# Attention and a mixture of experts on one core: one transpose block is moved to the head of its stage and to another bank, weight staging to POOL's queue, the query scale to ScalarE

## The chip, the core and the metric

The kernel runs on one core of a Trainium2 chip. The core has a matrix engine (TensorE, "PE" in the profile; its weight loads are listed apart as "PEld"), a vector engine (VectorE, "DVE"), an activation engine (ScalarE, "ACT"), a general engine (GpSimd, "POOL") and a sync engine (SyncE, "SP") that issues transfers; POOL issues transfers too. Engines run their own instructions in order and wait for each other through semaphores. PE writes its results into banks of an accumulator memory (PSUM), which VectorE and ScalarE read. The metric is the time of one execution in microseconds (us), as the device counts it.

## The reference

Causal attention by blocks of 64 over 8 batches of 8 heads, 576 positions, 64 values a head; its output rows, 512 wide, go through a layer of 8 experts with one expert to a row.

```python
scores = scale * np.matmul(q, k.transpose(0, 1, 3, 2))        # scale = 1/8
scores = np.where(block_i >= block_j, scores, -1e9)           # blocks of 64
attn = np.exp(scores - max); attn /= sum + 1e-9
attn_out = np.matmul(attn, v)                                 # x: rows of 8 heads, 4608 x 512
logits = x @ w_gate + modality_bias[modality_id]
e_idx = argmax(logits); gate_w = softmax(logits)[e_idx]
out[e_idx == e] = gate_w * (relu(x @ w1[e]) @ w2[e])
```

## The kernel before

**Attention** works on 32 pairs of heads, four pairs to a batch ("group" below). The program is written in 33 slots; slot s runs the steps of `ORDER` by hand, each engine taking its own steps in that order. A step's second number says how many pairs back it works: `("S0", 0)` is of pair s, `("Va", 1)` of pair s - 1, `("L", -2)` loads pair s + 2.

- `S0` to `S3`: scores (PE, line 197), 64x64 weights, into banks 0 to 5 by `PIECES`; `M0` to `M4`: row maxima (VectorE, 205 and 207); `E0` to `E4`: exponentials into `pm` (ScalarE, 213). `E4` reads banks 4 and 5 and is the last of the slot.
- `G`, `g`: the gate's products with v, and their copy; `L`: the load of a pair's queries and keys into `raw` (SP, 170). `Va`, `Vb` (PE, 247): the transposed weights of the pair before times v; `Za`, `Zb` (VectorE, 259 to 262): division and rows out; after every fourth pair two stores to `xrows` (SP, 265).
- `T0` to `T6` (PE, 223): transposes of `pm` in seven groups, the banks by `GBANK`; `T6` is the single block of the first 64 rows. `C0` to `C6` (228): copies out of the banks into `pt`, groups 1, 3 and 5 on VectorE, the others on ScalarE.
- `q...`: places where one step of a group's routing is run, of a list of 20 (logits, one-hot, counts, positions in the experts' row lists); `qp` takes steps that are small matmuls, `qv` those of VectorE that read them. Behind the routing of group 4 stand 22 further VectorE steps (`choose`, kind "c"), which pick the experts and the first rows.

`scale` multiplies a pair's queries by 1/8 into `q` (line 179): on POOL, at the start of the slot before the one that needs them. A slot's start also issues the loads of v (`load_v`, SP) and up to two scatters of list positions to `idlist` (POOL, 365), if any wait in `placing`.

**Early steps** of the experts lie in attention's last slots (`EARLY_STEPS`). `stage` loads a chunk of weights (128x1024; w1 in two halves) into one of two `staging` tiles; `prep` casts the oldest staged chunk on POOL (553), subtracts the cast from it for the low part (`lower`, 614) and stages the next. `ids` reads row numbers from `idlist` (SP, 626) after the scatters before it; `fetch` gathers rows of `xrows` (POOL, 634); `flush` issues all waiting scatters. Slot 32 (`LAST`) mixes the end of attention with the first expert products.

**Experts** (`run_all`): segments of 256 rows, each with transposes, w1 products (665), relu, w2 products (711) and scatters of the result (714, POOL), while further weight chunks are staged and converted (`convert`).

Of the kernel before, what the change touches and what calls it, by code (L numbers as in the profile page):

```python
# [16 lines left out]
ALU = mybir.AluOpType  # L17
# [5 lines left out]
B, H, S, D = 8, 8, 576, 64  # L23
# [31 lines left out]
    ((3, 0), (3, 1), (2, 0), (1, 0)), ((6, 3), (4, 2), (2, 1), (8, 4)), ((0, 0),),  # L55
)
HALF = 5
GBANK = (0, 1, 2, 3, 4, 5, 0)
POS = {x: 512 * g + 128 * i for g, group in enumerate(GROUPS) for i, x in enumerate(group)}
ON_DVE = (1, 3, 5)  # L60
PARTS = (("idf", (128,)), ("ii", (128,)), ("iom8", (NE,)), ("iom40", (5, NE)), ("iov40", (5, NE)), ("inv5", (5,)), ("first5", (NE, 5)), ("base8", (NE,)), ("edges", (N // SLOT,)))

ORDER = (
# [3 lines left out]
)  # L67

EARLY_STEPS = {
    (25, "S0"): ("ids", "stage", "stage"),  # L70
    (26, "S0"): ("prep",), (26, "T0"): ("prep",),
    (27, "S0"): ("prep",), (27, "T0"): ("prep",),
    (28, "S0"): ("prep",), (28, "T0"): ("prep",),
    (29, "S0"): ("prep",), (29, "T0"): ("prep",),
    (30, "S0"): ("fetch",),
    (31, "S0"): ("fetch",),
# [27 lines left out]
def attention_moe(ctx, tc, qk, vr, vt, gmw, mid, mb, w1, w2, cf, ci, ld, out):  # L104
# [71 lines left out]

    def scale(p):
        d = pairs[p]
        (pool if p else dve).tensor_scalar(d.q, d.raw[:, 0:S], SCALE, None, ALU.mult)  # L179

    def place(s, a, b):
        i, o = COL[s] if a == 0 else (COL[s][0] + 1, -CUT)
# [47 lines left out]
    def gates(p):  # L230
        d = pairs[p]
        for j in range(5):
            for i in range(2 if j < 4 else 1):
                k = 128 * j + 64 * i
                pe.matmul(b0[64 * i : 64 * i + 64, GATE + 2 * NE * j : GATE + 2 * NE * j + 2 * NE], d.vt[:, k : k + 64], gm[:, p % PPB, :], start=True, stop=True)
# [179 lines left out]

    def emit(name, p):
        one = {
            "L": lambda: load(p), "G": lambda: gates(p), "g": lambda: keep_gates(p), "Va": lambda: values(p, 0, SEVEN), "Vb": lambda: values(p, SEVEN, NSUB),
            "Za": lambda: rows(p, o0, 0, SEVEN), "Zb": lambda: rows(p, b0, SEVEN, NSUB),
        }  # L420
        if name in one:
            one[name]()
        else:
            dict(S=scores, M=maxima, E=exps, T=transposes, C=copies)[name[0]](p, int(name[1:]))
# [36 lines left out]
    def run_slot(slot):  # L461
        nonlocal steps, ex
        if slot < NPAIR - 1:
            load_v(slot + 1)
            scale(slot + 1)
        if placing and slot < NPAIR:
            for _ in range(2):
                if placing:
                    g, c = placing.pop(0)
                    g(c)  # L470
        for name, stage in LAST if slot == NPAIR else ORDER:
            p = slot - stage
            for what in EARLY_STEPS.get((slot, name), ()):
                if ex is None:
                    ex = Experts(ctx, tc, cst, scratch, btmp, con["edges"], xrows, idlist, idf, w1, w2, out, sel, run, base8, pick, dot, banks, (o0, banks[5]), placing, staging, extra, xrb)
                ex.early(what)
            if name[0:6] == "+steps":
                for f in steps[0 : int(name[6:])]:
                    f()
                steps = steps[int(name[6:]) :]  # L480
                continue
            if name[0] == "+":
                ex.early(name[1:])
                continue
            if name[0] == "q":
                kind = "" if name[1].isdigit() else name
                if slot > 1 and steps and getattr(steps[0], "kind", "") in ((kind, "c") if not kind else (kind,)):
                    steps.pop(0)()
                    if not kind and steps and getattr(steps[0], "kind", "") == "c":
                        steps.pop(0)()  # L490
                continue
            if not 0 <= p < NPAIR:
                continue
            emit(name, p)
            if name == "Zb" and p % PPB == PPB - 1:
                for f in steps:
                    f()
                steps = routing(p // PPB)
                if p // PPB == EARLY - 1:
                    choose(Later(dve, steps))  # L500
# [18 lines left out]
class Experts:  # L519
# [77 lines left out]
    def stage(self):  # L597
        if not self.todo:
            return
        k, name, c = self.todo.pop(0)  # L600
        st = self.staging[self.sturn % 2]
        self.sturn += 1
        if k == 0:
            for i in range(2):
                self.nc.sync.dma_start(st[64 * i : 64 * i + 64], self.source(k, name, c, i))
        else:
            st = st.rearrange("p (a f) -> p a f", a=2)
            self.nc.sync.dma_start(st, self.source(k, name, c))
        self.staged.append((st, k, name, c))

    def lower(self, on_pool=False):
# [254 lines left out]
```

## Time and profile before

| | us |
|---|---|
| median of 3 runs | 787.83 |
| lowest and highest of them | 787.63, 788.76 |
| the profiled execution | 790.35 |
| its span, first to last instruction | 788.7 |
| mean granted clock of TensorE | 0.988 |

Rows and timelines below are of the profiled execution, in us from the start of its span. A matmul's duration contains its way through the array, so matmuls that follow each other overlap; weight loads run beside matmuls. "issue" as the cause of an idle time means that the profile shows nothing that was waited for. A releaser is inferred, and of several it is the last one by the profile.

### The profile page before, as it was taken

The numbers are of one execution on the slowest core, as the hardware profiler recorded it, in microseconds if no ns is written. First come the engines' busy times: TensorE is split into PE (matmuls) and PEld (weight loads), VectorE is DVE, ScalarE is ACT, GpSimd is POOL, SyncE is SP. The second block draws the span as 40 slices with busy tenths as digits, with TensorE's granted clock in tenths as the row PEclk, the third lists the DMA queues.
The fourth block names the chain that finished last, engine by engine and source line by source line (L and its number), as shares of the span: only waits on it lengthen the run. The fifth ranks groups of instructions, "written<-read, shape, count | busy, mean of one in ns | idle before, by whom it ended". The sixth has DMA issues, their size and how long they took to land. (4 is left out here: it accounts for less than half of the span.)

```text
span 788.7 us, 20741 instructions
## 1 busy us (share of the span) xinstructions
PE 752.3 (95%) x8696; PEld 670.4 (85%) x8696; DVE 369.3 (47%) x1059; ACT 306.5 (39%) x654; POOL 216.5 (27%) x177
## 2 busy tenths in 40 slices
PE   8999999999989888799999999999999999999995
PEld 5888888888878876598999999999998889998894
DVE  6888888888879867654122111122212222212120
ACT  5666666666656654432222221222212222222221
POOL 2111323232323267621732322322222102112100
PEclk9999999999999999899999999999999999999998
DMA  8487565656554667623232112222122122121000
GB/s 236 120 224 218 142 166 144 168 148 165 148 161 126 179 176 225 159 67 85 48 92 81 63 46 81 68 81 68 54 81 81 54 68 68 54 68 45 27 14 19
DMA packets 82625, 85.11 MB, mean 108 GB/s; under 512 B 53003, under 2 KB 64971, under 8 KB 82529
## 3 DMA queue, kind: packets, MB, share of 16 engines
q1 hardware_dynamic: 75040, 64.24, 29.7%
q0 software_dynamic: 7488, 19.52, 7.8%
q8 instruction: 69, 1.13, 0.6%
q14 instruction: 28, 0.22, 0.1%
HBM read 62.09 MB, written 22.25 MB: 107 GB/s over the span
## 5 line engine op out<-in xcount | busy, mean ns | idle before, releaser
L672 DVE SCALAR_TENSOR_TENSOR extra<-bank,extra 128x512 fp32r<-128x512 f32 x72 | 49.8, 692 | 309.0 <-ACT extra L671 308.9
L213 ACT ACTIVATE pm<-bank,nm 128x320 f32<-128x320 f32 (+3 forms) x320 | 138.1, 507 | 89.7 <-DVE nm L205 88.2
L205 DVE TENSOR_REDUCE nm<-bank 128x1 f32<-128x256 f32 (+7 forms) x288 | 111.2, 446 | 39.4 <-PE bank L197 39.2
L665 PE MATMUL bank<-extra 128*128 128x256 f32 x960 | 117.7, 283 | 0.6 <-DVE extra L651 0.3
L665 PEld LDWEIGHTS bank<-extra 128*128 128x128 f32 x960 | 116.6, 192 | 1.7 <-DVE extra L651 0.5
L197 PE MATMUL bank<-raw,q 64*64 64x256 f32 (+7 forms) x1280 | 91.5, 426 | 19.9 <-POOL q L179 10.9
L179 POOL TENSOR_SCALAR q<-raw 128x576 f32<-128x576 f32 x31 | 51.2, 1650 | 212.7 <-DMA raw<-qk 124.5
L671 ACT ACTIVATE extra<-bank 128x512 fp32r<-128x512 f32 x72 | 43.1, 598 | 158.1 <-PE bank L665 158.1
L197 PEld LDWEIGHTS bank<-raw,q 64*64 64x64 f32 x1280 | 61.3, 138 | 49.0 <-issue 31.5
L223 PE MATMUL bank<-cf,pm 128*128 128x128 f32 (+1 forms) x800 | 94.8, 275 | 0.4 <-ACT pm L213 0.4
L665 PE MATMUL bank<-extra,w0hb 128*128 128x256 f32 x512 | 91.2, 281 | 0.0
L223 PEld LDWEIGHTS bank<-cf,pm 128*128 128x128 f32 (+1 forms) x800 | 85.8, 135 | 3.3 <-ACT pm L213 0.8
L228 ACT COPY pt<-bank 128x512 f32<-128x512 f32 (+1 forms) x128 | 62.7, 505 | 46.1 <-PE bank L223 46.1
L665 PEld LDWEIGHTS bank<-extra,w0hb 128*128 128x128 f32 x512 | 79.1, 188 | 0.7
L247 PE MATMUL o<-v,pt 128*64 128x73 f32 x2048 | 75.3, 228 | 1.6 <-issue 1.6
L247 PEld LDWEIGHTS o<-v,pt 128*64 128x64 f32 x2048 | 70.4, 136 | 1.8 <-issue 1.7
L665 PE MATMUL bank<-extra,w0lb 128*128 128x256 f32 x256 | 71.9, 281 | 0.0
L228 DVE COPY pt<-bank 128x512 f32<-128x512 f32 (+1 forms) x96 | 64.9, 684 | 9.5 <-PE bank L223 8.5
L714 POOL DMA_INDIRECT out<-scratch,ids_b x17 | 16.9, 994 | 162.2 <-ACT scratch L713 162.2
L711 PE MATMUL o<-extra 128*128 128x512 f32 x240 | 57.2, 394 | 0.0
L711 PE MATMUL bank<-extra 128*128 128x512 f32 x240 | 56.0, 389 | 0.0
L711 PEld LDWEIGHTS bank<-extra 128*128 128x128 f32 x240 | 45.1, 188 | 9.3
(144 smaller groups left out, 865.7 us busy)
## 6 DMA issues: line engine op xcount, KB each, us to landing
raw<-qk SPq DMA_DIRECT2D x31, 576.0 KB, 4.6
v<-vr SPq DMA_DIRECT2D x32, 320.0 KB, 5.4
vt<-vt SPq DMA_DIRECT2D x32, 288.0 KB, 5.3
xrows<-xr SPq DMA_DIRECT2D x16, 576.0 KB, 6.9
staging<-w SPq DMA_DIRECT2D x24, 256.0 KB, 3.9
staging<-w SPq DMA_DIRECT2D x12, 512.0 KB, 3.8
idlist<-btmp SPq DMA_DIRECT2D x8, 304.0 KB, 5.6
idlist<-idt,pi POOLq DMA_INDIRECT x40, 2.2
```

Of the source, the lines that this page charges most:

```text
L179: (pool if p else dve).tensor_scalar(d.q, d.raw[:, 0:S], SCALE, None, ALU.mult)
L197: pe.matmul(place(s, a, b)[64 * t : 64 * t + 64], d.q[hs, D * s : D * s + D], d.k[hs, a:b], start=True, stop=True)
L205: dve.tensor_reduce(low, place(s, a, b), AX.X, ALU.max, negate=True)
L213: act.activation(d.pm[:, OFF[s] + a : OFF[s] + b], place(s, a, b), AF.Exp, bias=d.nm[:, s : s + 1], scale=1.0)
L223: pe.transpose(banks[GBANK[g]][0:m, 128 * i : 128 * i + 128], d.pm[:, o : o + m], idf)
L228: dve.tensor_copy(dst, src) if g in ON_DVE else act.copy(dst, src)
L247: pe.matmul(o[64 * h : 64 * h + 64], d.pt[:, a : a + 64], d.v[:, 5 * h + j, :], start=j == 0, stop=j == s // 2)
L665: nc.tensor.matmul(hp[:, a, :], w[:, kc, ms], x[:, kc, :], start=i == 0, stop=i == len(mm) - 1)
L671: self.nc.scalar.activation(hh, hp, AF.Relu)
L672: self.nc.vector.scalar_tensor_tensor(hl, hp, 0.0, hh, ALU.max, ALU.subtract)
L711: nc.tensor.matmul(y, s.hs[m][x][:, ts], self.part(w, 1, m // 2)[:, m % 2, :], start=n == 0, stop=n == len(mm) - 1)
L714: nc.gpsimd.indirect_dma_start(self.out, bass.IndirectOffsetOnAxis(ap=s.ids[:, s.t + i : s.t + i + 1], axis=0), yo, None, bounds_check=N - ...
```

## The change

Four edits.

1. `T6` stands first among the transposes and writes bank 5 (`GBANK`); `C6` follows it.
2. `scale` of pairs 1 to 31 runs on ScalarE, as step `("Q", -1)` behind `E4`, that is, for the next pair; POOL no longer scales.
3. `stage` issues its loads from POOL's queue. `ids` moves from slot 25 to slot 28, behind a `flush`.
4. A `q` place takes one step; in the slots of group 5 (20 to 23, `EARLY`) it takes two.

```diff
-GBANK = (0, 1, 2, 3, 4, 5, 0)
+GBANK = (0, 1, 2, 3, 4, 5, 5)
...
-    ("G", 0), ("L", -2), ("q1", 1), ("Va", 1), ("g", 0), ("E4", 0), ("q2", 1), ("q3", 1), ("Vb", 1), ("Za", 1), ("q4", 1), ("Zb", 1),
...
+    ("G", 0), ("L", -2), ("q1", 1), ("Va", 1), ("g", 0), ("E4", 0), ("Q", -1), ("q2", 1), ("q3", 1), ("Vb", 1), ("Za", 1), ("q4", 1), ("Zb", 1),
+    ("T6", 0), ("C6", 0), ("T0", 0), ("C0", 0), ("T1", 0), ("C1", 0), ("T2", 0), ("C2", 0), ("q5", 1), ("T3", 0), ("C3", 0), ("T4", 0), ("C4", 0), ("T5", 0), ("C5", 0), ("qp", 1), ("q6", 1),
...
-    (25, "S0"): ("ids", "stage", "stage"),
+    (25, "S0"): ("stage", "stage"),
...
-    (28, "S0"): ("prep",), (28, "T0"): ("prep",),
+    (28, "S0"): ("flush", "ids", "prep"), (28, "T0"): ("prep",),
...
     def scale(p):
         d = pairs[p]
-        (pool if p else dve).tensor_scalar(d.q, d.raw[:, 0:S], SCALE, None, ALU.mult)
+        if p == 0:
+            dve.tensor_scalar(d.q, d.raw[:, 0:S], SCALE, None, ALU.mult)
+        else:
+            act.mul(d.q, d.raw[:, 0:S], SCALE)
...
             load_v(slot + 1)
-            scale(slot + 1)
...
-                if slot > 1 and steps and getattr(steps[0], "kind", "") in ((kind, "c") if not kind else (kind,)):
-                    steps.pop(0)()
-                    if not kind and steps and getattr(steps[0], "kind", "") == "c":
+                kinds = (kind,) if kind else ("", "c")
+                for _ in range(1 if kind or slot // PPB != EARLY else 2):
+                    if slot > 1 and steps and getattr(steps[0], "kind", "") in kinds:
                         steps.pop(0)()
...
-                self.nc.sync.dma_start(st[64 * i : 64 * i + 64], self.source(k, name, c, i))
+                self.nc.gpsimd.dma_start(st[64 * i : 64 * i + 64], self.source(k, name, c, i))
...
-            self.nc.sync.dma_start(st, self.source(k, name, c))
+            self.nc.gpsimd.dma_start(st, self.source(k, name, c))
```

In what follows a row of the program's order is a line, an operation, output<-input and the output's size; the changed file has its lines 2 or 3 lower. First PE, from the transposes of slot 1 to the scores of slot 2 (`bank_90` to `bank_95` are banks 0 to 5). Before:

```order
L223 MATMUL bank_90<-cf,pm_108 128x128 x4
L223 MATMUL bank_91<-cf,pm_108 128x128 x4
L223 MATMUL bank_92<-cf,pm_108 128x128 x4
L223 MATMUL bank_93<-cf,pm_108 128x128 x4
L223 MATMUL bank_94<-cf,pm_108 128x128 x4
L223 MATMUL bank_95<-cf,pm_108 64x128 x4
L223 MATMUL bank_90<-cf,pm_108 64x128
L197 MATMUL bank_90<-raw_98,q_100 64x512 x2
```

With the change:

```order
L226 MATMUL bank_95<-cf,pm_108 64x128
L226 MATMUL bank_90<-cf,pm_108 128x128 x4
L226 MATMUL bank_91<-cf,pm_108 128x128 x4
L226 MATMUL bank_92<-cf,pm_108 128x128 x4
L226 MATMUL bank_93<-cf,pm_108 128x128 x4
L226 MATMUL bank_94<-cf,pm_108 128x128 x4
L226 MATMUL bank_95<-cf,pm_108 64x128 x4
L200 MATMUL bank_90<-raw_98,q_100 64x512 x2
```

The single block has gone from the last to the first place and from bank 0 to bank 5, so that twenty transposes now lie between the last write to bank 0 and the next scores, which write it first.

Second ScalarE in slot 1, from its last four exponentials to the first of slot 2. Before:

```order
L213 ACTIVATE pm_108<-bank_94,nm 128x256 x2
L213 ACTIVATE pm_108<-bank_95,nm 128x320
L213 ACTIVATE pm_108<-bank_95,nm 128x128
L228 COPY pt_110<-bank_90 128x512
L228 COPY pt_110<-bank_92 128x512
L228 COPY pt_110<-bank_94 128x512
L228 COPY pt_110<-bank_90 64x128
L213 ACTIVATE pm_107<-bank_90,nm 128x512
```

With the change:

```order
L216 ACTIVATE pm_108<-bank_94,nm 128x256 x2
L216 ACTIVATE pm_108<-bank_95,nm 128x320
L216 ACTIVATE pm_108<-bank_95,nm 128x128
L182 ACTIVATE q_100<-raw_98 128x576
L231 COPY pt_110<-bank_95 64x128
L231 COPY pt_110<-bank_90 128x512
L231 COPY pt_110<-bank_92 128x512
L231 COPY pt_110<-bank_94 128x512
L216 ACTIVATE pm_107<-bank_90,nm 128x512
```

Between the last exponential and the copies stands now the scale of the next pair, and the 64x128 copy has gone from the last to the first of the copies.

Third SP's queue from slot 25's raw load on (`raw` loads pairs 27, 28; an ISA row sets an address). Before:

```order
L170 DMA raw_99<-qk 128x1152
L174 DMA vt_103<-vt 128x576
L175 DMA v_104<-vr 128x10x64
L605 ISA
L605 DMA staging_77<-w 64x1024
L605 ISA
L605 DMA staging_77<-w 64x1024
L170 DMA raw_98<-qk 128x1152
L605 ISA
L605 DMA staging_78<-w 64x1024
L605 ISA
L605 DMA staging_78<-w 64x1024
```

With the change, from slot 27's raw load (pair 29) to slot 28's (pair 30) and the stores that follow:

```order
L170 DMA raw_99<-qk 128x1152
L174 DMA vt_103<-vt 128x576
L175 DMA v_106<-vr 128x10x64
L627 TENSOR_LOAD di_a
L628 ISA
L628 DMA ids_lead<-idlist 128x6x1
L170 DMA raw_98<-qk 128x1152
L268 DMA xrows<-xr_79 64x9x256 x2
```

The stagings are gone from between the loads; the row ids of slot 28 now stand ahead of its raw load. The stagings stand on POOL. POOL before, from the scale of pair 29 to the preps of slot 29:

```order
L179 TENSOR_SCALAR q_101<-raw_99 128x576
L365 DMA idlist<-idt,pi 38912x16 x2
L553 CAST extra<-staging_77 128x1024
L614 TENSOR_TENSOR extra<-staging_77,extra 128x1024
L553 CAST extra<-staging_78 128x1024
L614 TENSOR_TENSOR extra<-staging_78,extra 128x1024
L179 TENSOR_SCALAR q_100<-raw_98 128x576
L365 DMA idlist<-idt,pi 38912x16 x2
```

With the change, from the preps of slot 27 to the first of slot 28:

```order
L555 CAST extra<-staging_77 128x1024
L616 TENSOR_TENSOR extra<-staging_77,extra 128x1024
L610 ISA
L610 DMA staging_77<-w 128x2x512
L555 CAST extra<-staging_78 128x1024
L616 TENSOR_TENSOR extra<-staging_78,extra 128x1024
L610 ISA
L610 DMA staging_78<-w 128x2x512
L368 DMA idlist<-idt,pi 38912x16 x5
L555 CAST extra<-staging_77 128x1024
L616 TENSOR_TENSOR extra<-staging_77,extra 128x1024
L610 ISA
```

Each lowering is followed by the transfer of the chunk after next, no scale is left, and the five scatters of slot 28's flush stand between the preps.

## Rows read from the trace of the kernel before

**Rows 1.** One line of the page: busy time of each engine, its share of the span, and its instructions.

```profile
PE 752.3 (95%) x8696; PEld 670.4 (85%) x8696; DVE 369.3 (47%) x1059; ACT 306.5 (39%) x654; POOL 216.5 (27%) x177
```

**Rows 2.** Busy time by stage. Columns: the stretch, its length, then for each engine busy time and (instructions), the granted share of TensorE's clock, the DMA engines' mean busy share, GB/s.

```profile
60.00:200.00 140.00, 135.22 (x2590) 120.28 (x2587) 118.60 (x383) 88.73 (x216) 38.64 (x30) 1.00 0.61 165
200.00:260.00 60.00, 56.10 (x1067) 49.24 (x1066) 51.31 (x178) 36.37 (x88) 18.47 (x15) 1.00 0.55 146
260.00:345.00 85.00, 70.47 (x1190) 60.06 (x1189) 61.17 (x183) 42.50 (x102) 49.47 (x35) 0.92 0.64 171
345.00:740.00 395.00, 395.00 (x2654) 360.58 (x2654) 86.00 (x170) 94.61 (x151) 94.79 (x83) 1.00 0.21 65
```

**Rows 3.** The timeline of slot 3 and of the start of slot 4. Columns: start, duration, engine, line, operation, output<-input, how many in a row, and in brackets the engine's idle time before and what ended it.

```profile
33.62 2.70 PE L197 MATMUL bank<-raw,q 64*64 64x512 f32 x40 [0.39 <-POOL q L179]
...
36.24 0.60 PEld L235 LDWEIGHTS b<-gm,vt 128*64 128x64 f32 x17 [0.17 <-issue]
...
36.38 0.33 SPq L170 DMA_DIRECT2D raw<-qk  x1
...
38.28 1.59 ACT L213 ACTIVATE pm<-bank,nm 128x256 f32<-128x256 f32 x4
...
40.17 2.68 PEld L223 LDWEIGHTS bank<-cf,pm 128*128 128x128 f32 x25
40.17 2.95 PE L223 MATMUL bank<-cf,pm 128*128 128x128 f32 x25
...
42.61 0.81 ACT L228 COPY pt<-bank 128x512 f32<-128x512 f32 x2 [0.23 <-PE bank L223]
43.12 0.68 DVE L228 COPY pt<-bank 64x512 f32<-64x512 f32 x1 [0.25 <-PE bank L223]
43.48 0.24 PEld L197 LDWEIGHTS bank<-raw,q 64*64 64x64 f32 x8 [0.63 <-issue]
43.52 2.70 PE L197 MATMUL bank<-raw,q 64*64 64x512 f32 x40 [0.40 <-issue]
...
44.70 1.82 DVE L205 TENSOR_REDUCE nm<-bank 128x1 f32<-128x512 f32 x4 [0.90 <-PE bank L197]
```

**Rows 4.** The costliest groups of the page, one row: the score matmuls; behind the bar, PE's idle time before them and what ended it.

```profile
L197 PE MATMUL bank<-raw,q 64*64 64x256 f32 (+7 forms) x1280 | 91.5, 426 | 19.9 <-POOL q L179 10.9
```

**Rows 5.** The timeline of PE alone from 250 to 345 us: the routing's small matmul at the end of slot 24, a stall within slot 26, the first scores of slots 27, 28, 30 and 31, and the first transposes of the expert stage.

```profile
254.07 0.44 PE L288 MATMUL b<-l,cf 128*128 128x72 f32 x2 [0.85 <-DVE l L285]
...
271.46 0.28 PE L247 MATMUL o<-v,pt 128*64 128x73 f32 x2 [1.57 <-issue]
...
276.23 2.70 PE L197 MATMUL bank<-raw,q 64*64 64x512 f32 x40 [0.34 <-issue]
...
288.05 4.38 PE L197 MATMUL bank<-raw,q 64*64 64x512 f32 x40 [2.33 <-POOL q L179]
...
312.23 4.39 PE L197 MATMUL bank<-raw,q 64*64 64x512 f32 x40 [2.95 <-POOL q L179]
...
329.43 4.41 PE L197 MATMUL bank<-raw,q 64*64 64x512 f32 x40 [5.24 <-POOL q L179]
...
340.99 1.09 PE L647 MATMUL bank<-cf,xr 128*128 128x128 f32 x8 [0.35 <-ACT pt L228]
```

**Rows 6.** The timeline of all engines in slot 30 and at the start of slot 31: staging and raw load on SP's queue (SPq), the scale on POOL, the scores on PE.

```profile
318.22 1.28 SPq L605 DMA_DIRECT2D staging<-w  x2
...
319.60 0.52 SPq L170 DMA_DIRECT2D raw<-qk  x1
...
327.72 1.65 POOL L179 TENSOR_SCALAR q<-raw 128x576 f32<-128x576 f32 x1 [6.11 <-DMA raw<-qk]
...
329.43 1.12 PE L197 MATMUL bank<-raw,q 64*64 64x512 f32 x4 [5.24 <-POOL q L179]
```

**Rows 7.** Busy time behind the wait of slot 28, columns as in rows 2.

```profile
288.60:291.90 3.30, 3.30 (x34) 2.13 (x30) 1.82 (x4) 1.44 (x4) 3.21 (x3) 0.50 0.02 5
```

**Rows 8.** The timeline of slot 5 (its scores start at 53.41): the last four exponentials, a step of the routing on VectorE, the transposes.

```profile
58.59 1.59 ACT L213 ACTIVATE pm<-bank,nm 128x256 f32<-128x256 f32 x4
...
59.05 0.19 DVE L298 TENSOR_REDUCE mx<-lg 128x5 f32<-128x40 f32 x1
...
60.09 2.95 PE L223 MATMUL bank<-cf,pm 128*128 128x128 f32 x25
```

**Rows 9.** The timeline of slot 0: its first 12 transposes, the last four exponentials, the transposes that waited for one of them.

```profile
9.63 1.53 PE L223 MATMUL bank<-cf,pm 128*128 128x128 f32 x12
...
10.58 1.56 ACT L213 ACTIVATE pm<-bank,nm 128x256 f32<-128x256 f32 x4
...
11.52 1.84 PE L223 MATMUL bank<-cf,pm 128*128 128x128 f32 x13 [0.36 <-ACT pm L213]
```

**Rows 10.** Groups of instructions, by shape: total busy time and mean ns behind the bar. ScalarE's cast of a weight chunk, and POOL's lowering and cast of one.

```profile
L614 POOL TENSOR_TENSOR extra<-staging,extra 128x1024 fp32r<-128x1024 f32 x8 | 18.9, 2362 | 0.7
...
L619 ACT CAST extra<-staging 128x1024 fp32r<-128x1024 f32 x8 | 8.5, 1063 | 0.0
L553 POOL CAST extra<-staging 128x1024 fp32r<-128x1024 f32 x8 | 8.4, 1049 | 0.0
```

**Rows 11.** The list-position scatters on POOL, of the tile pi: shortest, median and longest in ns, and first and last start.

```profile
L365 POOL DMA_INDIRECT idlist<-idt,pi x40: 967/988/1095, 81.8 to 381.5; - x40
```

**Rows 12.** The raw loads that SP issued from 250 to 345 us: time from issue to landing.

```profile
DMA to landing us min/median/max: 4.5/5.7/8.7
```

More of the change, by code (lines that the diff above doesn't have):

```diff
@@ L417, in emit @@
         one = {
-            "L": lambda: load(p), "G": lambda: gates(p), "g": lambda: keep_gates(p), "Va": lambda: values(p, 0, SEVEN), "Vb": lambda: values(p, SEVEN, NSUB),
+            "L": lambda: load(p), "Q": lambda: scale(p), "G": lambda: gates(p), "g": lambda: keep_gates(p), "Va": lambda: values(p, 0, SEVEN), "Vb": lambda: values(p, SEVEN, NSUB),
             "Za": lambda: rows(p, o0, 0, SEVEN), "Zb": lambda: rows(p, b0, SEVEN, NSUB),
```

1 row of the table ORDER is left out of this document.

## The prediction

> **What bounds the kernel now.** I read the page first, then the busy time by stage, then the timeline of one ordinary slot, then the odd slots. TensorE (PE) is busy for 752.3 of 788.7 us [rows 1], and the stages say where the rest is: from 345 to 740 us, the expert stage, it is busy 395.00 of 395 us, so no edit can gain there unless it removes matmuls, and this one removes none. In attention it is busy 135.2 of 140 us, then 56.1 of 60, then, from 260 to 345 us, only 70.5 of 85 with the mean granted clock at 0.92 [rows 2]. So I look for two things: a small wait in every slot, and large ones in the last slots.
>
> The ordinary slot shows the first. It begins with the scores at 33.62 us; the 25 transposes start at 40.17 (6.55 us into the slot), their weight loads end at 42.85 and the matmuls at 43.12; then PE waits 0.40 us (its weight loads 0.63) and the next slot's scores start at 43.52. Of ScalarE's two last copies (0.81 us from 42.61) the second ends at 43.42, just before [rows 3]. In the code that second copy is C6, which frees bank 0, and S0 writes bank 0. So each slot is 9.90 us, and its tail waits for a copy. Summed over slots the first matmul of the scores waited 19.9 us, 10.9 of them for POOL's scaled queries [rows 4].
>
> The second is those queries. In the late slots PE stood 2.33, 2.95 and 5.24 us before the scores of slots 28, 30 and 31, and each time the 40 score matmuls then took 4.38 to 4.41 us, where 2.70 is usual [rows 5]. The reason is SP's queue: weight staging stands in it ahead of the raw load, the staging waits for POOL's lowering of the previous chunk, so the load of slot 31's queries and keys left only at 319.60 us, in slot 30 itself, POOL scaled at 327.72 and PE started at 329.43 [rows 6]. After such a wait the granted clock is 0.50, the 1.2 GHz level [rows 7]; from 60 to 260 us it is 1.00 [rows 2].
>
> **The change, part by part.**
>
> *T6 first, into bank 5.* S0 now waits for C0, done long before, instead of C6. The gap before S0 is 0.40 us by matmuls and 0.63 by weight loads [rows 3]; both are bounds of what a boundary gives. I take 0.55: where nothing holds PE, the gates' weight loads come 0.17 us after those of the scores [rows 3], which leaves 0.46, and the scores may follow closer. 31 boundaries lie before slots 1 to 31; three of them are the query waits, counted below. 28 x 0.55 = 15.4 us. In 13 of these the routing's one or two small matmuls (kind "qp") stood inside the gap at no cost; at about 0.2 us a boundary (two matmuls, issued 0.11 apart as the 25 in 2.95 are) they now cost 2.6. **12.8 us.** The end of the last slot has the same wait, 0.35 us [rows 5]: **0.35**.
>
> What it costs: T6 writes bank 5, so it needs the slot's last exponential (E4), while the first transposes needed only earlier ones. In the ordinary slot E4 ends at 38.28 + 1.59 = 39.87, 0.30 us before the transposes start [rows 3]: covered, as everything else in the slot shifts with the scores. Where "qv" puts three small VectorE operations between the maxima (slots 5, 9, ... 29), E4 ends at 60.18 and the transposes start at 60.09 [rows 8]: with the 0.06 us that lie between the copy's end at 43.42 and the weight load at 43.48, 0.15 x 7 = 1.0 us lost. In slot 0 there is no cover (no values of an earlier pair): transposes began at 9.63, E4 ends at 10.58 + 1.56 = 12.14 [rows 9]. They will start near 12.2 and end 2.95 later at 15.15 instead of 13.36: 1.8 us lost. This opens a gap of 2.57 us; the gaps of 2.33 and more were followed by half clock, the one of 1.57 was not [rows 5], so it may cost another 0 to 1.7 us (the 4.38 less 2.70); I take 0.9. **Together 3.7 us given back.**
>
> *The scale on ScalarE.* POOL took 1.65 us; ScalarE's cast of 128x1024 between SBUF tiles takes 1.06 [rows 10], so 128x576 costs about 0.6. It stands between E4 and C6. ScalarE is busy 88.7 of 140 us [rows 2]; from E4's end (slot time 6.25) the scale ends at 6.9, the transposes' first bank is full at about 7.3, so C0 is not late. Cover: that wait for PE. Without it 0.6 us a slot, 19 us. What is queued behind it, if the raw load is late: all four copies, thus PE. In ordinary slots the load leaves SP at 36.38, 2.8 us into the slot [rows 3], and lands some 6 us later; ScalarE wants it at 9.35 + 6.25 = 15.6, 7 us after that.
>
> *Staging on POOL's queue.* SP then holds only loads of pairs, the xrows stores and the row ids. The raw loads leave in their slot, and the waits of 2.33 + 2.95 + 5.24 = **10.5 us** go, with the slow clock behind them, 1.68 + 1.69 + 1.71 = **5.1 us**. A stall of 1.57 us at 271.46 with no cause in the profile stands just behind the first burst of staging [rows 5]; it may go or stay: **0.8 of it**.
>
> POOL pays: 16 plain DMAs in attention (ten chunks, six of them in two halves). No row has such an issue from POOL; the nearest is a scatter of 128 rows, 0.97 to 1.10 us [rows 11], bounded below by nothing and above by that; I take 1.0 plus 0.3 between two. A chunk is then cast 1.05 + lowering 2.36 [rows 10] + one or two issues, 4.7 to 6 us. POOL runs ahead of the slots until the flush, which waits for group 5's list positions, about 7.5 us into slot 27. Before that stand four stagings and four preps, some 30 us from slot 24's middle: ready at slot 27's start, 5 us early. Five scatters end at slot 28 + 4.6 us, the last lands about 2.5 later, and only then can SP issue the row ids; behind them waits slot 30's raw load, at about slot 28 + 8.0. Landing takes 4.5 to 8.7 us, 5.7 in the middle [rows 12], so + 13.7; ScalarE wants it at E4's end of slot 29, + 16. Margin 2.3 us: no cost in the sum. After the flush come two chunks of 4.7 and two of 6 and the first two fetches, 2.6: slot 28 + 28.6; with 4.5 for landing the first rows are there at + 33, and are needed four slots on, at + 37.7.
>
> The Trainium skill's page "SBUF — State Buffer", section "SBUF: two separate sides", speaks against this edit: a DMA issued from POOL can't have its descriptors written while VectorE holds the shared port in a fast copy, so such loads belong on SP or ScalarE. Here the 40 scatters, most of them issued amid VectorE's copies in attention, lie within 0.97 to 1.10 us [rows 11], so the trace does not bear it out for these copies, which read PSUM; by the rule the issues would stretch, as in the last rival below.
>
> *Two steps at each q in slots 20 to 23, one elsewhere.* The same 42 steps, sooner. A step is about 0.19 us [rows 8]; twelve in a slot instead of six add 1.1 us to VectorE, which has 0.90 us idle before the next maxima [rows 3], and of that the faster slot takes 0.66. Slots 21 and 23 are full ones, so up to 1 us each reaches the next slot's E4; slot 24's flush keeps its wait of 0.85 us [rows 5] and perhaps 0.5 more. 0 to 3 us; I take **1.7 given back**.
>
> *Experts.* 20 of the stagings' issues move to POOL there, 20 us on an engine busy 94.8 of 395 [rows 2]; PE's segment has some 20 us, POOL's work in it about ten. Nothing.
>
> **Sum.** 12.8 + 0.35 + 10.5 + 5.1 + 0.8 = 29.5; less 3.7 and 1.7: 24.1 us. The profiled execution took 790.35 us around a span of 788.7; so it would take 766.2. The median before is 787.83, 2.5 lower, so I put the median after at 763.7.
>
> **Rivals.**
> 1. *The gap before S0 is not C6's.* If something as late holds S0 (the last transposes' own end), the boundaries give nothing: 24.1 less 13.1 is 11, 777 us. For it: the profile calls the wait "issue". Against: the copy's end lies 0.1 us ahead of S0 each time. 4%.
> 2. *VectorE becomes the bound.* It is busy 118.6 of 140 us [rows 2], 8.4 us of a slot that shall be 9.35. If its chain is 0.3 us too long in two thirds of the slots, 6 us go: 770 us. Against: 0.24 us stays before the maxima, and steps fill other idle places. 15%.
> 3. *POOL is late at the flush.* If issues or landings take 5 us more than the margins, slot 30's raw load holds ScalarE, its copies, then PE, and may slow the clock: 3 to 7 us, 767 to 771. 13%.
> 4. *Slower: POOL's issues are held by VectorE's work.* 21 issues lie before the first fetch. If each is held for three VectorE copies of 0.68 us [rows 3], 2 us, the fetch is 42 - 5 - 5 = 32 us late, 8 more than the gain: 796 us. It decides from about 1.6 us an issue. Against: [rows 11]. 3%. The skill's page above gives 3.1 us for an issue of 0.62 under a VectorE copy in its section "A bandwidth-pool intuition that's wrong (but worth ruling out)"; an estimate by it would be 2.5 x 21 - 34 = 18 us slower; no run here shows it.
> 5. *More than I say*: the full 0.63, no stall, no clock loss in slot 0, no cost of the early steps: 764 less 2.2, 0.8, 0.9 and 1.7, 758 us. 15%.
>
> **How the numbers follow.** The forecast has 50%, and its own range is 758 to 771 (0.40 instead of 0.55 costs 4.2 us, the clock 0.8, the stall 0.8, the steps 1.3). Rivals 2, 3 and 5 lie in or beside it. I give 757 to 772: outside are rivals 1 and 4, and some of 3. About 0.2% (1.6 us) is what a measurement here tells from no change. Faster: all but rival 4 and a mix of rivals that eats it up, 0.95; same 0.01; slower 0.04.
>
> **What would show it.** The scores start right behind the transposes' last weight load, slots of 9.3 to 9.5 us; no wait for POOL before the scores; clock 1.00 from 260 to 345 us; the first transposes at about 12.2 us; raw loads leave SP some 3 us into their slots, except slot 28's. Wrong would be: POOL's DMA issues well over 1.1 us, ScalarE waiting for the raw load in slot 29, or a wait of PE for VectorE at each slot's start.

## The result, and the profile after

The changed kernel takes 768.56 us (median of 4, 767.95 to 769.74), the kernel before 788.30 beside it (787.63 to 791.07): a ratio of 0.9745, 95% interval 0.9717 to 0.9772. The prediction was 763.7, from 757 to 772: the time lies inside, 4.9 us above the middle. The profiled execution took 769.74 us around a span of 768.1, 20.6 less than the span of before; the prediction's sum was 24.1.

That holds where these first profiles were taken. In the experiments, which ran on two chips, the kernel before takes 796.5 to 798.3 us, and on the one of them where the changed kernel ran again it takes 803.34 (800.15 to 808.90), ratio 1.0086 (1.0045 to 1.0128): there it is slower. Section 4 of the experiments shows where that time goes. The record does not name the chip of the first profiles; it is called the first chip below, the two others the second and the third. That another chip, and not another hour, makes the difference is inferred from the times. TensorE's clock is not the reason: the kernel before has a mean granted clock of 0.988 on the first chip and 0.989 on the third.

First two lines of the page, and the busy time by stage after (columns as in [rows 1, 2, 4]; the expert stage begins at 315.60):

```profile
PE 746.2 (97%) x8696; PEld 663.8 (86%) x8696; DVE 366.2 (48%) x1059; ACT 323.1 (42%) x685; POOL 188.8 (25%) x182
...
L200 PE MATMUL bank<-raw,q 64*64 64x256 f32 (+7 forms) x1280 | 86.6, 408 | 0.0
```

```profile
60.00:200.00 140.00, 139.51 (x2673) 121.74 (x2672) 122.98 (x400) 99.90 (x239) 17.85 (x19) 1.00 0.64 171
200.00:260.00 60.00, 59.29 (x1154) 51.49 (x1147) 54.86 (x192) 42.61 (x102) 19.03 (x20) 1.00 0.74 192
260.00:315.60 55.60, 53.84 (x1038) 47.38 (x1033) 49.38 (x156) 38.31 (x93) 35.28 (x31) 1.00 0.73 201
```

The 19.9 us that the scores had waited [rows 4] are 0.0, PE is busy for 139.51 of 140 us instead of 135.22, and the late slots run at a clock of 1.00 instead of 0.92 [rows 2]. Slot 3, with the start of slot 4, shows the new boundary; it answers to [rows 3]:

```profile
35.74 2.70 PE L200 MATMUL bank<-raw,q 64*64 64x512 f32 x40
...
38.52 0.33 SPq L170 DMA_DIRECT2D raw<-qk  x1
...
40.42 1.58 ACT L216 ACTIVATE pm<-bank,nm 128x256 f32<-128x256 f32 x4
...
41.89 0.69 ACT L182 ACTIVATE q<-raw 128x576 f32<-128x576 f32 x1
...
42.30 2.92 PE L226 MATMUL bank<-cf,pm 128*64 128x128 f32 x25
42.63 0.26 ACT L231 COPY pt<-bank 64x128 f32<-64x128 f32 x1
...
44.87 0.59 ACT L231 COPY pt<-bank 128x512 f32<-128x512 f32 x1 [0.29 <-PE bank L226]
...
45.15 0.21 PEld L200 LDWEIGHTS bank<-raw,q 64*64 64x64 f32 x8 [0.20 <-issue]
45.15 0.65 PE L200 MATMUL bank<-raw,q 64*64 64x512 f32 x4
```

The small copy C6 ends at 42.89, the scores start at 45.15 while C4 still runs (to 45.46), 0.20 us behind the last weight load: 9.40 us a slot instead of 9.90. The scale (41.89) stands in ScalarE's wait for PE. Slot 0 answers to [rows 9]; PE first, then the exponentials, then busy time with the granted clock:

```profile
12.43 4.58 PE L226 MATMUL bank<-cf,pm 128*64 128x128 f32 x25 [2.16 <-ACT pm L216]
```

```profile
10.81 1.56 ACT L216 ACTIVATE pm<-bank,nm 128x256 f32<-128x256 f32 x4
```

```profile
12.40:17.00 4.60, 4.58 (x29) 4.38 (x30) 1.38 (x2) 2.26 (x5) 0.00 (x0) 0.63 0.76 228
```

The transposes wait for E4 to 12.37 and then run, mostly at the 1.2 GHz level (granted clock 0.63 over the stretch), for 4.58 us instead of 2.92. Last the end: the last scatter in the timeline, and the DRAIN instructions of POOL's sequencer at the end of the program (shortest, median and longest in ns, then the first and the last start; the longest is the first); both after, then both before:

```profile
755.41 0.98 POOL L716 DMA_INDIRECT out<-scratch,ids_c  x1 [4.41 <-ACTq L794]
```

```profile
L864 POOLq DRAIN  x3: 46/103/5869, 761.4 to 767.8; - x3
```

```profile
780.88 0.97 POOL L714 DMA_INDIRECT out<-scratch,ids_c  x1 [4.41 <-ACTq L792]
```

```profile
L862 POOLq DRAIN  x3: 46/103/3097, 784.8 to 788.4; - x3
```

The last scatter starts 25.47 us earlier, the span ends only 20.6 earlier. Between the scatter and the longest drain lie 5.99 us instead of 3.88, and that drain takes 5.87 instead of 3.10: 4.9 us that the sum did not hold. Where the time went, by slot lengths of the two traces (the starts of the scores):

| | predicted gain | measured |
|---|---|---|
| start, slot 0 | -2.2 | -0.2, -2.9 |
| slots 1 to 26 without 21 (boundaries, qv, stall of 26, steps) | 10.6 + 0.8 - 1.7 | 9.8 |
| slot 21 | 0.4 | 1.9 |
| slots 27 to 31 (waits, clock, boundaries) | 16.2 | 16.8 |
| expert stage, first transposes to last product | 0 | 0.1 |
| from the last scatter on | 0 | -4.9 |

### The profile page after: what moved, and what is told of

The parts are those of the page before. It is cut to its first block, busy times and chain, and to the rows that moved or that the text cites. A ratio compares the mean times of both kernels' runs of the same rounds, so it can differ in the third digit from the quotient of the medians.

```text
span 768.1 us, 20749 instructions
## 1 busy us (share of the span) xinstructions
PE 746.2 (97%) x8696; PEld 663.8 (86%) x8696; DVE 366.2 (48%) x1059; ACT 323.1 (42%) x685; POOL 188.8 (25%) x182
## 3 DMA queue, kind: packets, MB, share of 16 engines
q0 software_dynamic: 11136, 32.11, 13.8%
## 5 line engine op out<-in xcount | busy, mean ns | idle before, releaser
L368 POOL DMA_INDIRECT idlist<-idt,pi x40 | 39.7, 992 | 227.8 <-DVE inv L263 186.5
L200 PE MATMUL bank<-raw,q 64*64 64x256 f32 (+7 forms) x1280 | 86.6, 408 | 0.0
L200 PEld LDWEIGHTS bank<-raw,q 64*64 64x64 f32 x1280 | 53.9, 133 | 29.5 <-issue 18.9
L231 ACT COPY pt<-bank 128x512 f32<-128x512 f32 (+1 forms) x128 | 64.5, 504 | 28.5 <-PE bank L226 27.5
L713 PE MATMUL o<-w1b,extra 128*128 128x512 f32 x216 | 52.5, 398 | 0.0
```

Source lines behind the costliest of these rows:

```text
L200: pe.matmul(place(s, a, b)[64 * t : 64 * t + 64], d.q[hs, D * s : D * s + D], d.k[hs, a:b], start=True, stop=True)
L231: dve.tensor_copy(dst, src) if g in ON_DVE else act.copy(dst, src)
L368: last = pool.indirect_dma_start(idlist[:], bass.IndirectOffsetOnAxis(ap=g.pi[:, c : c + 1], axis=0), g.idt[:, c, :], None, bounds_check=N ...
L713: nc.tensor.matmul(y, s.hs[m][x][:, ts], self.part(w, 1, m // 2)[:, m % 2, :], start=n == 0, stop=n == len(mm) - 1)
```

## Experiments

The kernels ran in three groups of four, each on one chip ("call" in an expectation means such a group): sections 1 and 2 on the second chip, the rest on the third. A ratio is to the kernel before in the same group.

**1. The boundary.** `t6_alone` is the kernel before with `GBANK` and the two `ORDER` lines of the change.

> The kernel before with the first edit alone: T6 first among the transposes and into bank 5. If C6 was what held the next scores, the slots up to 26 take 9.40 us (about 9.6 where the routing's small matmuls stand at the boundary), which gains 10.4 us over slots 1 to 26 as in the changed kernel, slot 0 loses 2.9, the end of the last slot gives 0.35; the waits for POOL's queries in slots 28 to 31 stay and may grow by what those slots got shorter. About 780 us. If the gap before the scores is not C6's (first rival), the slots stay at 9.90 us and only slot 0's loss is left: about 791 us.

789.43 us, ratio 0.9903 (0.9868 to 0.9937): 7.1 us faster, 8 expected. Slot 0 takes 10.72 us, slots 1 to 3 9.40, slot 4 9.58: the same as in the changed kernel, so edit 1 alone makes the boundary. The gap was C6's; the first rival falls. The waits for POOL's queries stay, 10.0 us (the last number is what was waited for them):

```profile
L197 PE MATMUL bank<-raw,q 64*64 64x256 f32 (+7 forms) x1280 | 91.9, 428 | 10.0 <-POOL q L179 10.0
```

`t6_last_bank3` is the changed kernel with T6 and C6 behind C5 in `ORDER` again, and in a bank that the next scores write last:

```diff
-GBANK = (0, 1, 2, 3, 4, 5, 5)
+GBANK = (0, 1, 2, 3, 4, 5, 3)
```

> The changed kernel with T6 last again, but into bank 3, which the next scores write only in their last unit. If what counts is which bank C6 has to free, and not that T6 comes first, ordinary slots stay at 9.40 us with T6 last; slot 0 no longer waits for its last exponential, so its 4.58 us of transposes at half clock and its late start go (2.9 + 0.5 us), and the slots whose last exponential is late (5, 9, 10, 13, 17, 21, 22, 25, 29, 30) give about 2 us more, since T6 no longer needs it first. Together 5.4 us: about 763 us. Rival: T6 at the end must wait for VectorE's copy C3 out of bank 3, 0.3 us in each slot: 768.6 + 9 - 3.4, about 774 us.

803.72 us, 1.0086 (1.0059 to 1.0113): it has the pauses of section 4 (slot 8 takes 13.82 us), so only the slots without them tell the theories apart. Slot 0 takes 7.48 us instead of 10.72, ordinary slots 9.54: between the two. So the bank is what frees the boundary, and T6's place costs slot 0. T6 does wait for C3 on VectorE, by half of what the rival said; the slots with a late E4 gain nothing by T6 coming last (slot 5 takes 9.68 us in both):

```profile
41.70 0.11 PEld L226 LDWEIGHTS bank<-cf,pm 128*64 128x64 f32 x1 [0.18 <-DVE pt L231]
```

**2. The end.** `load_experts_sp` stages through POOL's queue only in attention, `load_rest_sp` everywhere but in the closing loop (`rest`), which runs no turn; the last line stands ahead of `run_all` in the one and ahead of `rest` in the other:

```diff
+        self.queue = self.nc.gpsimd
...
-            self.nc.gpsimd.dma_start(st, self.source(k, name, c))
+            self.queue.dma_start(st, self.source(k, name, c))
...
+        ex.queue = nc.sync
```

> The changed kernel, but only the staging loads that lie in attention (10 chunks, 16 loads) stay on POOL's queue; those of the expert stage and of the closing loop go back to SP's. TensorE's work ended 25.5 us earlier in the changed kernel, its span by only 20.6: the stretch from the start of the last scatter to the end of the span is 12.7 us there and 7.8 before, and 2.8 of the difference is a longer last drain of POOL (5.87 against 3.10 us). Theory A: the drain grows with the number of loads that POOL has issued, so 16 instead of 36 leave 3.10 + 2.77 x 16/36 = 4.3 us, and the loop's own part (2.1 us) goes: about 765 us. Theory B: it is only the closing loop, whose body (it runs no turn) holds POOL's loads: the stretch is 7.8 us again, about 763.7 us. Theory C: neither: 768.6 us. Nothing else moves by more than 0.5 us.

> The changed kernel, but the staging loads in the body of the closing loop, which runs no turn, go back to SP's queue; all 36 that are executed stay on POOL's. Theory A (the last drain of POOL grows with the loads it issued): the drain stays at 5.9 us, the loop's own part of 2.1 us goes: about 766.5 us. Theory B (the closing loop alone lengthens the end): the stretch from the last scatter to the end is 7.8 us as before: about 763.7 us. Theory C: 768.6 us.

796.12 us, 0.9997 (0.9973 to 1.0022), and 798.20, 1.0021 (0.9996 to 1.0046): on that chip neither is told from before, and only the ends of their traces answer. POOL's longest drain in each, first `load_experts_sp`, then `load_rest_sp`:

```profile
L866 POOLq DRAIN  x3: 46/103/4240, 791.2 to 796.0; - x3
```

```profile
L866 POOLq DRAIN  x3: 46/103/5869, 790.7 to 797.1; - x3
```

Theory A holds. With 118 transfers issued by POOL (before) the drain takes 3.10 us, with 134 4.24 (4.3 expected), with 154 5.87 whether the loop holds loads or not: 0.07 us for each of the first 16 staging loads, 0.08 for each of the other 20. By bytes the two steps agree better: the pages give 19.52, 24.77 and 32.11 MB for the queue of POOL's transfers (`software_dynamic`), 0.22 us for each MB more in both. So it seems to go with what was moved and not with the number of transfers, but no run separates the two. The stretch from the last scatter to the end is 7.82, 9.06 and 10.39 us, 12.68 in the changed kernel: the loop's loads add 2.3 by themselves, without one being executed. Of these, 1.89 us are one semaphore instruction of POOL's sequencer at the loop (line 794); in the other three no such instruction takes more than 0.04. What it waits for is not shown.

**3. Which edit frees the queries.** `load_all_sp` undoes edit 3 (staging on SP's queue, `ids` in slot 25 without a flush); `scale_pool` undoes edit 2 (step `Q` leaves `ORDER`):

```diff
-            act.mul(d.q, d.raw[:, 0:S], SCALE)
+            pool.tensor_scalar(d.q, d.raw[:, 0:S], SCALE, None, ALU.mult)
...
             load_v(slot + 1)
+            scale(slot + 1)
```

> The changed kernel with the third edit undone: staging loads on SP's queue again, the row ids back in slot 25. Theory of the prediction (SP's queue is what makes the queries late): the waits of 10.5 us before the scores of slots 28, 30 and 31 and the 5.1 us at half clock come back, now by way of ScalarE's scale, which waits for the raw load with four copies behind it, and the end is 4.9 us shorter: the changed kernel of this call plus 10 us. Rival (the scale on POOL was the other half of it: POOL's casts and lowerings waited behind the scale, the staging on SP behind the lowering, and the raw load behind the staging; without the scale POOL runs ahead): no such wait, and the shorter end alone is left: the changed kernel of this call less 4.9 us.

> The changed kernel with the second edit undone: POOL scales the queries of the next pair at each slot's start, the rest as changed. POOL then has in slots 26 to 29 two preps of 4.7 to 6 us and a scale of 1.65 us in each slot of 9.4 us: late by 2 to 4 us a slot, so TensorE waits for the queries in slots 28 to 31, 10 to 15 us with the slow clock behind it: the changed kernel of this call plus 10 us. Rival: POOL has enough in hand before slot 26 and nothing is late: the same as the changed kernel within 2 us. Where scatters in a row hold up all engines (as in the last call), the scale spreads them two to a slot, and slots 8 to 20 go back to 9.6 us, which alone would give 12 us.

`load_all_sp`: 796.69 us, 0.9990 (0.9970 to 1.0010), 6.7 less than the changed kernel beside it; `scale_pool`: 790.31, 0.9926 (0.9902 to 0.9951). What the scores waited for, first in `load_all_sp`, then in `scale_pool` (its groups, and the longest wait in its timeline):

```profile
L200 PE MATMUL bank<-raw,q 64*64 64x256 f32 (+7 forms) x1280 | 89.5, 408 | 2.7 <-ACT pt L231 1.9 <-issue 0.7
```

```profile
L200 PE MATMUL bank<-raw,q 64*64 64x256 f32 (+7 forms) x1280 | 88.0, 414 | 3.7 <-POOL q L182 3.7
```

```profile
304.61 4.39 PE L200 MATMUL bank<-raw,q 64*64 64x512 f32 x40 [2.54 <-POOL q L182]
```

With the staging back on SP no score waits for a query; ScalarE's scale waited for a raw load twice, 0.7 us together. So the rival holds: it was the scale on POOL that closed the ring (raw load behind staging, staging behind lowering, lowering behind scale, scale behind raw load). On this chip, where the kernel before waits 11.3 us for its queries (`before_again`), edit 2 opens the ring alone; edit 3 alone leaves 3.7 us and one start at half clock. Neither was tried alone on the first chip. `scale_pool` is the fastest of its group all the same, since its slots 8 to 20 have no pauses (section 4); its slot 29 has, and takes 17.39 us.

**4. The pauses.** `changed_again` is the changed kernel itself, `before_again` the kernel before. `paced` puts a small copy on POOL that needs a maximum of the running slot ahead of each scatter up to slot 27:

```diff
+AFTER = {"M1": 7, "M4": 1}
...
+            if name in AFTER and placing and slot < 28:
+                pool.tensor_copy(gate, pairs[p].nm[:, AFTER[name] : AFTER[name] + 1])
+                g, c = placing.pop(0)
+                g(c)
```

> The changed kernel as it is, on the chip of this call, so that the others have it beside them. In the last call the kernel before took 796.5 us instead of 788, and in the two kernels there that issue loads as the changed one does, the slots 8, 12, 16 and 20 took 12.1 to 13.5 us and slot 24 17.5 to 17.8, where the changed kernel's first profile has 9.58 and 10.38: all engines pause while POOL issues four or five scatters, 1.3 us apart. Theory A (it goes with that chip): on such a chip about 798 us, otherwise 768.6 us with slots of 9.58. Theory B (it goes with the two variants' loads): 768.6 us on any chip.

> The changed kernel, but up to slot 27 each scatter of list positions follows a copy of 128x1 on POOL that needs a maximum of the running slot (the first after M1, the second after M4), so that two scatters lie some 3.5 us apart instead of four or five in a row at 1.3 us. Theory (scatters in a row hold up all engines on some chips): where the changed kernel has slots 8, 12, 16 and 20 at 12.4 us and slot 24 at 17.6, they fall to 9.6 and to 10.5 to 13 us: 16 us less than the 803.3 us of the last call, about 787; where the changed kernel has none of these (its first profile), 768.6 us within 1. Rival (the pauses belong to ScalarE's scale or to POOL's loads): the slots stay at 12.4 us.

> The kernel before, for a profile of it on the chip of this call. If it is one of the chips where POOL's transfers in a row hold up the engines, slots 8, 12, 16 and 20 stay at 9.90 us (two scatters and a scale to a slot), and the 8 us that it takes longer there lie where POOL issues four gathers or more in a row: in slots 30 and 31 and in the expert stage, which took 444 to 446 us there from its first transposes to the last product instead of 438.9. Otherwise 788 us with the expert stage at 438.9.

`changed_again` 803.34 us, `paced` 787.02 (786.59 to 788.39; about 787 expected), 0.9864 (0.9846 to 0.9881), `before_again` 797.60 in one run. Slot lengths in us, from the starts of the scores, and the expert stage from its first transposes to the last product:

| | slot 3 | 8 | 12 | 24 | 28 | 30 | experts |
|---|---|---|---|---|---|---|---|
| before, first chip | 9.90 | 9.90 | 9.90 | 10.72 | 11.59 | 17.20 | 438.9 |
| before_again | 9.90 | 9.89 | 10.06 | 10.55 | 10.29 | 16.03 | 444.7 |
| changed, first chip | 9.40 | 9.58 | 9.58 | 10.38 | 9.58 | 9.99 | 438.8 |
| changed_again | 9.40 | 12.45 | 12.40 | 17.60 | 12.45 | 14.90 | 444.6 |
| paced | 9.40 | 9.75 | 9.77 | 11.06 | 13.71 | 16.82 | 444.3 |
| best2 (below) | 9.40 | 9.76 | 9.81 | 11.03 | 10.67 | 15.28 | 444.3 |

The timeline of slot 8's start in the changed kernel, POOL's last two scatters of five, VectorE's maxima and PE, on the first chip:

```profile
83.27 2.70 PE L200 MATMUL bank<-raw,q 64*64 64x512 f32 x40
...
84.46 3.14 DVE L208 TENSOR_REDUCE nm<-bank 128x1 f32<-128x512 f32 x8 [0.33 <-PE bank L200]
...
85.31 0.98 POOL L368 DMA_INDIRECT idlist<-idt,pi  x1 [0.30 <-issue]
...
85.89 0.70 PE L238 MATMUL b<-gm,vt 128*64 128x16 f32 x17
...
86.59 0.99 POOL L368 DMA_INDIRECT idlist<-idt,pi  x1 [0.30 <-issue]
```

and in `changed_again`:

```profile
83.20 2.96 PE L200 MATMUL bank<-raw,q 64*64 64x512 f32 x40
...
85.23 0.98 POOL L368 DMA_INDIRECT idlist<-idt,pi  x1 [0.31 <-issue]
...
86.08 0.23 PE L238 MATMUL b<-gm,vt 128*64 128x16 f32 x1
86.52 0.18 PE L238 MATMUL b<-gm,vt 128*64 128x16 f32 x1 [0.20 <-issue]
86.52 0.98 POOL L368 DMA_INDIRECT idlist<-idt,pi  x1 [0.30 <-issue]
...
87.24 0.27 PE L238 MATMUL b<-gm,vt 128*64 128x16 f32 x3 [0.55 <-issue]
87.26 0.76 DVE L208 TENSOR_REDUCE nm<-bank 128x1 f32<-128x448 f32 x2 [2.16 <-PE bank L200]
...
88.65 0.59 PE L238 MATMUL b<-gm,vt 128*64 128x16 f32 x13 [1.14 <-issue]
```

The same scatters at the same times; on the third chip PE's gate products stretch from 0.7 to 3.2 us with nothing that the profile shows them waiting for, and VectorE stands for 2.16 us beside them. With two scatters to a slot, 3 us apart (`paced`), the slot takes 9.75 us; with two in a row and a scale (`scale_pool`) 9.58. `load_all_sp`, which stages nothing through POOL, has the same five scatters and 12.43 us, so it is not POOL's loads. On the second chip the same: slot 8 takes 13.54 us in `load_experts_sp`, which issues as the changed kernel does, and 9.58 in `t6_alone`, where POOL scales. So it is scatters that POOL issues in a row, on these two chips. `before_again` agrees: two scatters and a scale to a slot cost at most 0.2 us in attention; in the expert stage nine transfers stand in a row from 372.55 us, PE pauses four times beside them (2.7 us), and the stage takes 5.8 us more than on the first chip. All of that lies there: from 370 to 390 us PE is busy for 17.06 of 20 us at a granted clock of 0.91, on the first chip, beside the same nine transfers, for 20.00 at 1.00. What inside the chip holds the engines, no run shows.

In slot 24 one thing follows from the other. Delayed by the pauses, the choosing steps on VectorE (line 95) fall beside POOL's lowering; lowering and one of them in `changed_again`, and the same step on the first chip:

```profile
260.22 2.35 POOL L616 TENSOR_TENSOR extra<-staging,extra 128x1024 fp32r<-128x1024 f32 x1
...
260.81 1.78 DVE L95 TENSOR_TENSOR rest<-taken,cf 128x8 f32<-128x8 f32 x1
```

```profile
243.96 0.15 DVE L95 TENSOR_TENSOR rest<-taken,cf 128x8 f32<-128x8 f32 x1
```

The step ends with the lowering (262.59 and 262.57), 1.78 us instead of 0.15. The Trainium skill's page "SBUF — State Buffer", section "SBUF: two separate sides", says that a VectorE operation with two inputs in SBUF and a GpSimd operation that reads SBUF take one port pair in turns, each for its whole length; this row agrees.

**5. Two steps at a q.** `steps_single` puts the old rule of edit 4 back.

> The changed kernel with the fourth edit undone (a q place takes one step, and one more if the next is of kind c). The prediction put a price of 1.7 us on the edit, which would come back: 1.7 us less than the changed kernel. The trace of the changed kernel says 0.2: its slot 22 has 0.1 to 0.2 us more, slots 21, 23 and 24 nothing. Rival: on a chip with pauses the steps of kind c come later, beside POOL's lowerings, which stretch them to 1 to 2.3 us each: slot 24 or 25 then takes some us more than the changed kernel's 17.6.

802.86 us, 1.0062 (1.0032 to 1.0092), against 1.0086 for the changed kernel: not told apart. Slot 22 takes 9.46 instead of 9.57 us, slot 24 12.72 instead of 17.60, slot 26 10.69 instead of 9.46; the rival, a longer slot 24, did not come. The 0.1 us is the trace's price; that 1.7 is not, is read from the first chip's slots 21, 23 and 24 (9.67, 9.40, 10.38), which lost nothing. On the third chip the pauses cover the question.

**6. Better versions.** `best` is the changed kernel with T6 last, in bank 3, in slot 0 alone, and staging as in `load_experts_sp`.

> The changed kernel with two things altered: in slot 0 alone T6 stands last, in bank 3 (slot 0 then takes about 7.5 us instead of 10.7), and the staging loads of the expert stage and of the closing loop go through SP's queue (16 loads stay on POOL's). Theory: 3.2 us in slot 0, and of the 4.9 us that the end has grown about 3.6 if the drain goes with the number of loads that POOL issued, all 4.9 if it goes with the closing loop: the changed kernel of this call less 6.8 to 8.1 us. Rival: slot 0's clock stays low all the same, or the end does not shrink: less than 3.5 us.

797.22 us, 1.0002 (0.9978 to 1.0025): 6.1 less than the changed kernel beside it, 6.8 to 8.1 expected. Slot 0 takes 7.47 us and the stretch behind the last scatter 8.91, 3.2 and 3.8 us less; ordinary slots keep 9.40, and the pauses stay.

`best2` stages through SP everywhere, reads the row ids in slot 26, keeps slot 0's order of `best`, and paces all scatters and each second gather of slots 30 and 31.

> The first two edits and the fourth, staging on SP's queue as before (row ids in slot 26), in slot 0 T6 last in bank 3, all scatters paced as in the paced kernel, and of the two gathers in slots 30 and 31 the second paced too. Theory: slot 0 gives 3.2 us, the end 4.8, no query is late (as with the staging on SP in the last call), and no engine pauses up to slot 31: on a chip like that of the last two calls 803 - 11.3 (slots 8 to 20) - 7 (24) - 2.9 (28) - 5 (30) - 8.0, about 769 us, on one like the first profile's 768.6 - 8.0, about 760.6 us. Rival: the queries are late again behind the staging in slots 28 to 31, 10 us more.

776.71 us (776.32 to 777.27), 0.9739 (0.9721 to 0.9756): 21.6 us faster than before and 26.6 than the changed kernel, both on that chip; 769 was expected. Of what is missing, 5.4 us lie in slot 30, which was to lose 5 and still takes 15.28 with four transfers close together; slots 21 and 26 take 1.4 and 1.5 us more than in the changed kernel, around a stall of 1.2 to 1.3 us in each, and slot 28 gives 1.8 of 2.9. It beats both kernels where it ran; on the first chip it did not run.

## Why the prediction was right, and where not

- **What bounds the kernel.** Right: small waits at each boundary and large ones in the last slots; both are gone, and the expert stage did not move (438.9 and 438.8 us).
- **The boundary** of 0.55 measured 0.50, 0.32 where two f32 routing matmuls stand (0.2 predicted for them, 0.18 measured), 0.44 where two bf16 ones do. In the qv slots E4 is later: 10.03 became 9.68, a gain of 0.35, so 0.15 lost, as taken. Together 0.7 us less than the sum had, 0.25 of it in slot 13 alone (9.93).
- **VectorE** did not become the bound (rival 2): ahead of the maxima of slot 8 it still waits 0.33 us for PE.
- **Slot 0.** The mechanism was right (12.2 predicted, 12.43 measured, then half clock), the clock's term was too small: 1.66 us of the 1.7 that the bound allowed, 0.9 taken.
- **The queries.** The 15.6 us came, with clock 1.00. But the working put them on the staging's move; by the runs of the third chip they are the scale's. That the sum came out is luck: both edits are in the change. Taken apart they would have been forecast wrong: by the prediction's theory `load_all_sp` was to lose 10 us, and it lost none.
- **POOL's issues.** 0.56 us (halves) and 0.77 (whole chunks) instead of 1.0. All 36 lie between 0.53 and 0.78, so none was held for the 2 us of rival 4; it falls on the first chip. Its slower time came on the third by another way: there the engines pause beside POOL's scatters, and POOL's staging issues stay as short (0.53 to 0.78).
- **The flush.** Slot 30's raw load left 6.9 us into slot 28 (8.0 predicted), the first two gathers were through at slot 28 + 29.3 (28.6); no engine waited for either. Rival 3 falls on the first chip.
- **The double steps** cost about 0.1 us, 1.7 were taken. **The stalls**: that of slot 26 stayed (1.63 us), that of slot 21 went. `before_again` lacks it too (slot 21 takes 10.03 us), so it is not the change's: 1.5 us of the gain are luck.
- **What failed** is "Experts. ... Nothing". For 20 issues it asked only where they would stand beside PE's work, and not what the program does with POOL's queue behind the last product: 4.9 us, which with 1.3 us more than forecast in attention and 0.1 in the expert stage makes 20.6 of 24.1. The term that stood at nothing measured 4.9 us, 2.8 in POOL's longest drain and 2.1 ahead of it.

## What to carry to other kernels

When transfers move to another engine's queue, read the end of the span too: what is paid there for the queue's use is in no stage of the work. A ring of waits (load, staging, lowering, scale) can open at one link; try which is cheapest before moving a queue. Here the scale alone was enough, the queue alone was not. And work that stood between an engine's transfers also spaced them: taking it away can cost more than it gave, in one place and not in another.

## What was not expected of the hardware

- POOL's longest drain takes 3.10 us after 118 transfers of its queue (19.52 MB), 4.24 after 134 (24.77 MB) and 5.87 after 154 (32.11 MB).
- Loads in the body of a loop that runs no turn lengthened the end by 2.3 us (12.68 against 10.39).
- Beside five scatters in a row, 1.3 us apart, PE and VectorE pause, and the slot grows by some 2.9 us on the second and third chip; in the first profiles the same five cost nothing.
